# Late softmax probabilities moved by way of DRAM instead of from SBUF to SBUF

## The chip, the cores and the metric

The kernel runs on one core of one Trainium2 chip. The metric is device microseconds of one execution; lower is better.

## The reference

Three layers follow one another over 4 x 576 = 2304 tokens of 512 numbers. The first is attention with 8 heads, half of them with a local mask and half with a strided one, the second a dense squared-ReLU layer, the third a layer of 8 experts of which each token uses one:

```python
scores = np.where(masks, scale * q @ k.T, -1e9)     # local: 32 back; strided: same position mod 32
attn = softmax(scores) @ v                          # (B, H, S, D) = (4, 8, 576, 64)
x = attn.transpose(0, 2, 1, 3).reshape(2304, 512)
h = np.maximum(x @ w_in, 0.0)                       # 512 -> 2048
x = (s * (h * h) + b) @ w_out                       # 2048 -> 512
e = argmax(x @ w_gate, axis=1)                      # one expert per token
out = p[e] * sigmoid(x @ w_output_gate)[e] * (relu(x @ w1[e]) @ w2[e])   # 512 -> 1024 -> 512
```

## The kernel before

All work is written as generators (`attn`, `moe1`, `load_qkv` and so on). A planner, `Order.run`, keeps a clock for each engine, looks at which step could start first by its estimated cost and its rank (the `prio` of `spawn`; a lower number goes first), and so writes one fixed list of instructions for each engine. On the chip every engine runs its list in order and waits on semaphores. The constants such as `DMA_LAT` and `PH_LAT` are the planner's guesses of when a transfer lands; they set the order and no wait.

Tokens are cut into five units (256, 512, 512, 512, 512). Attention is cut into 23 rounds (`GROUPS`). Rounds 0 to 8 come first (lines 591 to 757) and are followed by the dense layer of unit 0; rounds 9 to 22, the late ones, are laid between the products of the dense layer (L1095 into `h`, L1129 from `g`), so that TensorE always has something to do. A late round is one visit on TensorE: 16 products of probabilities with v (L884, from `phs`), and right behind them the scores of the round two further on (L799). Those scores go through the mask (L818), the maximum (L842), the exponentials on ScalarE (L849), the division (L855) and 32x32 transposes on VectorE (L859) into the one tile `prt`. From there the blocks have to come to other partitions, in the one tile `phs`, which has its zeros from the start. In the kernel before, eight DMAs of 32 KB, from SBUF to SBUF, do this (four in rounds of half width); they may start when the products of the round before have read `phs`.

All DMAs of the kernel but a few are issued by SyncE (SP), in the order of its list: also the loads of q, k (`qkv`, 128 x 1088) and v (128 x 1024) of the late rounds, which have one buffer each, the raw weights of the dense layer (`raw64`, in 64-bit words), and `xp`, in which the partial result of a unit is put aside (L1512) and fetched back (L1520) through one tile `x1`. A wait in front of one of them holds up all that stand behind it.

At the start, while attention has not filled TensorE yet, the generator `warm` puts in products of zeros, whose result nobody reads. From L1091 on TensorE works without them.

Of the kernel before, what the change touches and what calls it, by code (L numbers as in the profile page):

```python
# [6 lines left out]
F32 = mybir.dt.float32  # L7
# [29 lines left out]
P = 128  # L37
STRIDE = 32
QB = 64
# [13 lines left out]
NPR = 2  # L53
QG = 32
NQE = 6
P_CHAIN = -0.35
P_ATT = -0.3
# [17 lines left out]
P_ATT2 = 0.1  # L75
# [45 lines left out]
def dims(g):  # L121

    if GROUPS[g][0] == "L":
        return (QB, LK) if g < NEARLY else (QG, 2 * QG)
    j0, j1, r = part_of(g)
    if g >= NEARLY:
        return r * (j1 - j0), r * j1
    return r * (j1 - j0), QB if GROUPS[g][0] == "P" else r * j1


def span(g):
    kind, b, i0, n = GROUPS[g]
    if kind == "L":
        return b * S + i0 * QB, b * S + (i0 + n) * QB
    j0, j1, _ = part_of(g)
    return b * S + j0 * STRIDE, b * S + j1 * STRIDE
# [61 lines left out]
LAT = 0.25  # L198
DMA_LAT = 1.8
LATE_LAT = 0.8  # L200
PH_LAT = 0.8
BIG = 180


# [112 lines left out]
def op(*engs, waits=(), dep=True, on=(), late=0.0):  # L317
    return engs, waits, dep, on, late
# [6 lines left out]
def body(ctx, tc, qkv, w12, moe_s, moe_b, wg, e12, out):  # L325
    nc = tc.nc
# [5 lines left out]
    dram = enter(tc.tile_pool(name="dram", bufs=1, space=DRAM))  # L332
# [23 lines left out]
    prs = [at.tile([P, 1024 // 2], F32, name=f"pr{k}", tag=f"pr{k}", bufs=1) for k in range(NPR)]  # L356
    prt = at.tile([P, 1024 // 2], F32, name="prt", tag="prt", bufs=1)
    phs = at.tile([P, 2, 2, 256], F32, name="phs", tag="phs", bufs=1)
    away = at.tile([P, 2, USZ[AWAY]], F32, name="away", tag="away", bufs=1)
    mh = wp.tile([P, sum(MB[0])], F32R, name="mh", tag="w")  # L360
    x0 = wp.tile([P, KD, USZ[0]], F32, name="x0", tag="w")
# [26 lines left out]
    zero = xk["S"][:, 1, 1, COL["S"][2]:COL["S"][2] + 2 * P]  # L388
# [6 lines left out]
    o = Order()  # L395
# [68 lines left out]
    t_qe, t_qk, t_vv, t_pt, t_ph = Tok(NQE), Tok(1), Tok(1), Tok(1), Tok(1)  # L464
# [108 lines left out]
    for g, (kind, b, i0, n) in enumerate(GROUPS):  # L573
        t0, t1 = span(g)
# [229 lines left out]
    def late_mask(g, sc, toks):  # L804
        kind, b, i0, n = GROUPS[g]
        local = kind == "L"
        nq, w = dims(g)
        m = 2 * n
        sm = at.tile([P, 24], F32, name="sm", tag="sm", bufs=NSM)
        ps4 = prs[g % NPR][:, 0:m * 2 * QG].rearrange("p (h i k) -> p h i k", h=2, k=2 * QG)[:, :, :, 0:w]  # L810
        edge = [i for i in range(n) if local and (i0 + i) % NLB == 0]
        some = [(i, i + 1, ml[:, 2 * QG:4 * QG]) for i in edge]
        for i, j in zip([0] + [i + 1 for i in edge], edge + [n]):
            if i < j:
                some.append((i, j, ml[:, 0:2 * QG] if local else late_m[kind, b]))
        yield op(("DVE", m * w / 960 + 0.15 * len(some)), on=toks)
        for i, j, mask in some:
            nc.vector.tensor_tensor(out=ps4[:, :, i:j], in0=sc[:, :, i:j], in1=mask.unsqueeze(1).unsqueeze(1).to_broadcast([P, 2, j - i, w]), op=ALU.add)  # L818
        o.spawn(late_rest(g, sm, ps4), prio=P_ATT2, pe=P_ATT)

    def attn_late(g):
        n = GROUPS[g][3]
# [9 lines left out]
    def late_rest(g, sm, ps4):  # L832
        kind, b, i0, n = GROUPS[g]
        local = kind == "L"
        nq, w = dims(g)
        m = 2 * n
# [8 lines left out]
        for h in range(2):  # L845
            for i in range(n):
# [10 lines left out]
        nb = 2 if w > QG else 1  # L857
        yield op(("DVE", nb * m * QG / 960 + 0.15), waits=[t_pt])
        nc.vector.transpose(out=prt[:, 0:nb * m * QG].rearrange("p (b c q) -> p b c q", b=nb, q=QG),  # L859
                            in_=pr[:, 0:m * 2 * QG].rearrange("p (c b q) -> p b c q", b=2, q=QG)[:, 0:nb])  # L860
        o.free(t_p)
        yield op(("DMA", 2.55 * nb), waits=[t_ph])
        for x in range(2):
            for y in range(nb):
                for p in range(2):
                    a, r = p * QB + x * QG, x * QB + y * QG
                    nc.sync.dma_start(out=phs[r:r + QG, p, x, 0:m * QG], in_=prt[a:a + QG, y * m * QG:(y + 1) * m * QG])
        t1 = o.fin + DMA_LAT + PH_LAT
        o.free(t_pt, t1)
        ev = Ev()  # L870
        o.set(ev, t1)
        tot = m * nq
# [7 lines left out]
        for i in range(n):  # L880
            for p in range(2):
                for h in range(2):
                    c = (h * n + i) * QG
                    nc.tensor.matmul(out=two[h * D:(h + 1) * D, p, 256 + 2 * i * nq:256 + 2 * (i + 1) * nq], lhsT=vv[:, i, p, h, :],  # L884
                                     rhs=phs[:, p, :, c:c + nq])
        o.free(t_vv)
        o.free(t_ph)
        if nx:
# [3 lines left out]
        for t0, c, z, _ in segs:  # L892
            if local:
                a = t0 - span(g)[0]
# [7 lines left out]
        for z, src, dst, u in runs:  # L902
            if u == AWAY:
# [9 lines left out]
                if local:  # L913
                    a = span(g)[0] - UOF[AWAY]
# [13 lines left out]
        if nx:  # L928
            yield from late_mask(nx, sc, toks)
# [1370 lines left out]
    def extra(col, get, n=NT):  # L2300
        yield op(("DMA", 4.2), waits=[ev_gid])
        e = get()
        gr = mx.tile([1, SLOT], I32, name="gr", tag="gr", bufs=1)
        gc = mx.tile([P, 2], I32, name="gc", tag="gc", bufs=1)
        with nc.allow_non_contiguous_dma(reason="one column of a table"):
            nc.sync.dma_start(out=gr, in_=col(gid).rearrange("s o -> o s"))
            for h in range(NROW):
                nc.sync.dma_start(out=gc[h * SLOT:(h + 1) * SLOT, 0:1], in_=col(gid))
            nc.sync.dma_start(out=gc[0:SLOT, 1:2], in_=col(sid))
        t_gr = Ev()  # L2310
        o.set(t_gr, o.fin + 3.0)
        yield op(("DVE", 0.4), waits=[t_gr])
        gs = mx.tile([P, 3], I32, name="gs", tag="gs", bufs=1)
        nc.vector.tensor_single_scalar(out=gs[:, 0:1], in_=gc[:, 0:1], scalar=P - 1, op=ALU.bitwise_and)
        nc.vector.tensor_single_scalar(out=gs[:, 1:2], in_=gc[:, 0:1], scalar=P.bit_length() - 1, op=ALU.logical_shift_right)
        nc.vector.scalar_tensor_tensor(out=gs[:, 2:3], in0=gs[:, 0:1], scalar=float(NQT), in1=gs[:, 1:2], op0=ALU.mult, op1=ALU.add)
        yield op(("POOL", 1.1))
        se = mx.tile([P, 1], F32, name="se", tag="se", bufs=1)
        nc.gpsimd.indirect_dma_start(out=se, out_offset=None, in_=scd,
                                     in_offset=bass.IndirectOffsetOnAxis(ap=gs[:, 2:3], axis=0))  # L2320
        src = mx.tile([P, KD, NT], F32, name="X1", tag="big", bufs=1)
        for u in range(NU):
            yield op(("DMA", USZ[u] / 180), waits=[ev_last[u], ev_raw])
            nc.sync.dma_start(out=src[:, :, UOF[u]:UOF[u + 1]], in_=xd[u])
        ev = Ev()
        o.set(ev, o.fin + DMA_LAT + 1.0)
        yield op(("DVE", 1.8), waits=[t_r, ev])
        xe = mx.tile([P, KD, SLOT], F32, name="xe", tag="r", bufs=NR)
        for k in range(0, SLOT, 4):
            if k:  # L2330
                yield op(("DVE", 0.8))
            _, vs = nc.values_load_multi_w_load_instructions(
                gr[0:1, k:k + 4], engines=[DVE], min_val=0, max_val=NT - 1, skip_runtime_bounds_check_because=why)
            for j, v in enumerate(vs):
                nc.vector.tensor_copy(out=xe[:, :, k + j:k + j + 1], in_=src[:, :, bass.ds(v, 1)])
        big = mx.tile([P, NF2, 1024], F32, name="we", tag="big", bufs=1)
        we = []
        evs = []
        for fc in range(NF2):
            yield op(("DMA", 1.46))  # L2340
            t = big[:, fc, :]
            nc.sync.dma_start(out=t, in_=e12[bass.ds(e * NF2 + fc, 1)].rearrange("o p f -> p (o f)"))
            we.append(t)
            evs.append(Ev())
            o.set(evs[-1], o.fin + DMA_LAT)
        if n < NT:
            yield op(("DMA", 0.5))
            ex["lrow"] = const.tile([1, P], I32, name="lrow")
            nc.sync.dma_start(out=ex["lrow"], in_=lsd.rearrange("(o s) c -> o (s c)", o=1))
        if n < NT:  # L2350
            oe = yield from rows_fast(xe, we, evs, se)
        else:
            oe = rows_short(xe, big, se)
        ex["oe"], ex["gc"] = oe, gc
        if n < NT:
            yield from merge_rows(oe, gc)
        yield op(("POOL", 1.1), waits=list(ev_out))
        nc.gpsimd.indirect_dma_start(out=out[0:n], out_offset=bass.IndirectOffsetOnAxis(ap=gc[0:SLOT, 1:2], axis=0),
                                     in_=oe, in_offset=None, bounds_check=n - 1, oob_is_err=False)
        o.free(t_g)  # L2360
# [13 lines left out]
    def warm():  # L2374
        yield op(("PE", 0.0), waits=[t_l1])
        t = ps.tile([P, 512], F32, name="warm", tag="l1")
        n = 0
        while ev_x[0].t is None and n < WARM:
            yield op(("PE", 0.155), dep=False)
            nc.tensor.matmul(out=t[:, 0:2 * P], lhsT=zero[:, 0:P], rhs=zero)  # L2380
            n += 1
        o.free(t_l1)

# [126 lines left out]
```

## Time and profile before

| what | value |
|---|---|
| time, median of 3 runs | 663.77 us (661.78 to 665.29) |
| the profiled execution's own time | 662.37 us |
| its span, first to last instruction | 660.6 us |
| TensorE busy | 651.9 us, 99% of the span |
| VectorE, ScalarE busy | 426.6 us, 312.8 us |
| mean granted TensorE clock | 0.997 |
| DMA share, first slices and mean GB/s | 0.8 to 0.9 in the first two slices of 40; 127 GB/s over the span |

The span is 1.77 us shorter than the execution's own time. "Busy" on TensorE counts a product from its start to its modelled end, so that products that overlap are counted once; an engine that is busy for 99% of the span has hardly any moment without a product under way.

### The profile page before, as it was taken

Reading aid. Unit: us, or ns where it says so; the run is one execution under the profiler, and the core shown is the slowest. Engines: PE = TensorE matmul, PEld = TensorE weight load, DVE = VectorE, ACT = ScalarE, POOL = GpSimd, SP = SyncE. Lnnn points to the kernel's source line nnn. Section 1 sums busy time; section 2 is a strip of 40 time slices with the busy share of each in tenths; the row PEclk is TensorE's granted clock in tenths of the full one; section 3 lists DMA queues with packets and bytes.
Section 4 is the critical chain, followed back from the end, with each engine's and each line's share of the span. In section 5 each row is a group of like instructions: output and inputs, shape, how many; then the busy total and the mean of one; then the engine's idle time right before and its main releaser. Section 6 shows DMA issues by size and latency. Waiting matters only on the chain. (4 is left out here: it accounts for less than half of the span.)

```text
span 660.6 us, 14155 instructions
## 1 busy us (share of the span) xinstructions
PE 651.9 (99%) x5424; PEld 570.0 (86%) x5424; DVE 426.6 (65%) x1001; ACT 312.8 (47%) x848; POOL 38.8 (6%) x135
## 2 busy tenths in 40 slices
PE   7999999999999999999999999999999999999997
PEld 6888888899878888898899889988899999998996
DVE  5898868776545557566575767887687566535540
ACT  4876865677566444353243464543322423314311
POOL 7650000000000000000000000000000000000000
PEclk9999999999999999999999999999999999999999
DMA  8982356673544232112211242333220660910201
GB/s 312 405 334 96 112 209 208 207 245 103 177 152 169 81 106 65 49 48 97 87 50 42 64 152 68 116 97 96 96 65 2 177 237 14 327 44 16 81 1 66
DMA packets 40823, 83.81 MB, mean 127 GB/s; under 512 B 6701, under 2 KB 20142, under 8 KB 39986
## 3 DMA queue, kind: packets, MB, share of 16 engines
q1 hardware_dynamic: 40658, 82.87, 37.2%
q8 instruction: 43, 0.70, 0.5%
q14 instruction: 26, 0.21, 0.1%
q0 software_dynamic: 96, 0.02, 0.0%
HBM read 64.11 MB, written 15.63 MB: 121 GB/s over the span
## 5 line engine op out<-in xcount | busy, mean ns | idle before, releaser
L1095 PE MATMUL h<-xsl,w 128*128 128x512 f32 (+1 forms) x492 | 109.5, 369 | 0.0
L1129 PE MATMUL bk<-g,w 128*128 128x512 f32 (+1 forms) x480 | 105.5, 368 | 0.0
L1190 PE MATMUL bk<-g,w 128*128 128x512 f32 x396 | 102.2, 393 | 0.0
L1095 PEld LDWEIGHTS h<-xsl,w 128*128 128x128 f32 x492 | 84.8, 188 | 15.6 <-issue 0.4
L1968 PE MATMUL bk<-w,ht 128*128 128x512 f32 x384 | 96.0, 391 | 0.0
L1129 PEld LDWEIGHTS bk<-g,w 128*128 128x128 f32 x480 | 83.0, 188 | 14.7
L1190 PEld LDWEIGHTS bk<-g,w 128*128 128x128 f32 x396 | 69.9, 188 | 11.6
L1968 PEld LDWEIGHTS bk<-w,ht 128*128 128x128 f32 x384 | 68.6, 188 | 11.6
L1043 ACT ACTIVATE r<-h 128x512 f32<-128x512 f32 (+1 forms) x48 | 25.3, 528 | 62.5 <-PE h L1095 59.5
L1069 DVE TENSOR_TENSOR g<-r,g 128x512 fp32r<-128x512 f32 (+1 forms) x41 | 26.0, 633 | 42.6 <-ACT g L1067 42.2
L1442 PEld LDWEIGHTS h<-xsl,w 128*128 128x128 f32 x336 | 45.5, 190 | 3.8 <-issue 0.2
L1442 PE MATMUL h<-xsl,w 128*128 128x256 f32 x336 | 47.0, 283 | 0.0
L1873 ACT ACTIVATE ht<-h 128x256 fp32r<-128x256 f32 x24 | 9.2, 385 | 73.2 <-PE h L2010 47.0
L849 ACT ACTIVATE pr<-pr,sm 128x64 f32<-128x64 f32 (+2 forms) x102 | 32.8, 322 | 0.3
L1914 DVE TENSOR_TENSOR dd<-h,su 128x256 f32<-128x256 f32 x16 | 6.8, 424 | 29.5 <-PE h L2010 29.4
L1356 ACT ACTIVATE g<-dd 128x512 fp32r<-128x512 f32 x16 | 10.1, 631 | 31.5 <-DVE dd L1349 31.5
L1067 ACT ACTIVATE g<-r 128x512 fp32r<-128x512 f32 (+1 forms) x41 | 23.9, 583 | 1.7
L1055 ACT ACTIVATE r<-r 128x512 f32<-128x512 f32 (+1 forms) x41 | 23.9, 584 | 1.1
L2010 PE MATMUL bk<-x,wc 128*128 128x256 f32 x168 | 24.4, 281 | 0.0
L1442 PE MATMUL h<-xsl,s 128*128 128x256 f32 x168 | 24.3, 279 | 0.0
L1442 PEld LDWEIGHTS h<-xsl,s 128*128 128x128 f32 x168 | 22.6, 188 | 1.3
L1938 ACT ACTIVATE ob<-bk,scl 128x512 f32<-128x512 f32 x17 | 11.7, 689 | 23.5 <-PE bk L1968 22.8
(306 smaller groups left out, 1132.7 us busy)
## 6 DMA issues: line engine op xcount, KB each, us to landing
raw<-w SPq DMA_DIRECT2D x32, 512.0 KB, 6.9
qkv<-qkv SPq DMA_DIRECT2D x14, 512.0 KB, 4.7
xr<-xd SPq DMA_DIRECT2D x9, 512.0 KB, 4.7
qkv<-qkv SPq DMA_DIRECT2D x8, 544.0 KB, 6.3
out<-ob SPq DMA_DIRECT2D x17, 256.0 KB, 2.1
xd<-x SPq DMA_DIRECT2D x4, 1024.0 KB, 4.2
sraw<-sd SPq DMA_DIRECT2D x16, 256.0 KB, 2.7
wraw<-e SPq DMA_DIRECT2D x16, 256.0 KB, 3.0
```

The source lines that it names most:

```text
L849: nc.scalar.activation(out=ps4[:, h, i, :], in_=ps4[:, h, i, :], func=AF.Exp, scale=0.125, bias=v[2][:, j:j + 1], accum_out=v[1][:, j:j + 1])
L1043: nc.scalar.activation(out=r, in_=h, func=AF.Relu)
L1055: nc.scalar.activation(out=to, in_=r, func=AF.Square)
L1067: nc.scalar.activation(out=gt[:, 0, 0:U], in_=r, func=AF.Copy)
L1069: nc.vector.tensor_sub(out=gt[:, 1, 0:U], in0=r, in1=gt[:, 0, 0:U].bitcast(F32))
L1095: nc.tensor.matmul(out=h, lhsT=w_t[2 * fc][:, a, c * P:(c + 1) * P], rhs=xt(u, c, x), start=(c == 0 and n == 0), stop=(c == KD - 1 and n = ...
L1129: nc.tensor.matmul(out=acc[pu][c], lhsT=w_t[2 * pf + 1][:, a, c * P:(c + 1) * P], rhs=gt[:, x, 0:cols(pu)], start=(first and n == 0), stop ...
L1190: nc.tensor.matmul(out=acc[pu][c], lhsT=w_t[2 * pf + 1][:, a, c * P:(c + 1) * P], rhs=pbox[0][:, x, 0:cols(pu)], start=(begin and i == 0), ...
L1442: nc.tensor.matmul(out=out_, lhsT=weights(x, a, c), rhs=o_place(u, b)[y][:, c], start=(first and c == 0 and n == 0), stop=(name in ("M2", ...
L1938: nc.scalar.activation(out=ob, in_=src, func=AF.Copy, scale=scl[:, i:i + 1])
L1968: nc.tensor.matmul(out=acc2[s, t][0], lhsT=box[k][:, x, t * P:(t + 1) * P], rhs=w_t["p", 2 * f + 1][:, a, :], start=(f == 0 and n == 0), s ...
L2010: nc.tensor.matmul(out=banks[to], lhsT=t[:, a, off + c * P:off + (c + 1) * P], rhs=x2[s, b][:, y, c, :], start=(first and c == 0 and n == ...
```

## The change

The late probabilities go from `prt` to a DRAM tile (`ptd`, two of them) in two DMAs, and from there into `phs` in four (two for rounds of half width), whose axes are swapped. The loads wait until the stores have landed. `prt` is free when the stores have landed, and no longer when `phs` has been filled. The planner gets other numbers: two issues at 1.15 us and four at 1.74 us in place of eight at 5.1 us, 0.4 us more for the stores' landing than for a plain one, `PH_LAT` 1.0 for 0.8, 2.0 us more for the landing of the expert weights of the extra rows, and rank -0.1 instead of 0.1 for the work behind the scores of rounds 14 and later. Each warming product of 256 columns becomes two of 128; the planner counts 0.155 us for the pair as it did for the one.

```diff
-PH_LAT = 0.8
+PH_LAT = 1.0
+G_ATT3 = 14
+P_ATT3 = -0.1
+PS_LAT = 0.4
+WE_LAT = 2.0
...
+    ptd = [dram.tile([2, QG, 2, 2, 256], F32, name=f"ptd{k}") for k in range(NPR)]
...
-        o.spawn(late_rest(g, sm, ps4), prio=P_ATT2, pe=P_ATT)
+        o.spawn(late_rest(g, sm, ps4), prio=P_ATT3 if g >= G_ATT3 else P_ATT2, pe=P_ATT)
...
-        yield op(("DMA", 2.55 * nb), waits=[t_ph])
+        yield op(("DMA", 1.15))
+        pd_ = ptd[g % NPR]
+        c = m * QG
+        for p in range(2):
+            nc.sync.dma_start(out=pd_.rearrange("x k b p c -> (x k) b p c")[:, 0:nb, p, 0:c],
+                              in_=prt[p * QB:(p + 1) * QB, 0:nb * c].rearrange("q (b c) -> q b c", b=nb))
+        t1 = o.fin + DMA_LAT + PS_LAT
+        o.free(t_pt, t1)
+        ev = Ev()
+        o.set(ev, t1)
+        yield op(("DMA", 0.87 * nb), waits=[t_ph, ev])
         for x in range(2):
-            for y in range(nb):
-                for p in range(2):
-                    a, r = p * QB + x * QG, x * QB + y * QG
-                    nc.sync.dma_start(out=phs[r:r + QG, p, x, 0:m * QG], in_=prt[a:a + QG, y * m * QG:(y + 1) * m * QG])
+            for b in range(nb):
+                nc.sync.dma_start(out=phs[x * QB + b * QG:x * QB + (b + 1) * QG, x, :, 0:c], in_=pd_[x, :, b, :, 0:c])
         t1 = o.fin + DMA_LAT + PH_LAT
-        o.free(t_pt, t1)
...
-                                     rhs=phs[:, p, :, c:c + nq])
+                                     rhs=phs[:, :, p, c:c + nq])
...
-            o.set(evs[-1], o.fin + DMA_LAT)
+            o.set(evs[-1], o.fin + DMA_LAT + WE_LAT)
...
             yield op(("PE", 0.155), dep=False)
-            nc.tensor.matmul(out=t[:, 0:2 * P], lhsT=zero[:, 0:P], rhs=zero)
+            for c in (0, P):
+                nc.tensor.matmul(out=t[:, c:c + P], lhsT=zero[:, 0:P], rhs=zero[:, c:c + P])
```

In the list of TensorE, the change moves the late rounds among the products of the dense layer and leaves their number as it is. Here is round 10 before (L1095 and L1129 are the dense layer, L884 and L799 the round):

```order
L1095 MATMUL h<-xsl,w 128x512 x12
L1129 MATMUL bk_937<-g,w 128x512 x3
L1129 MATMUL bk_938<-g,w 128x512 x3
L1129 MATMUL bk_939<-g,w 128x512 x3
L1129 MATMUL bk_940<-g,w 128x512 x3
L884 MATMUL bk_1177<-phs,qkv 64x48 x16
L799 MATMUL bk_1177<-qkv 32x64 x32
```

And the same place in the changed kernel, in which L1107 and L1141 are the dense layer, L896 and L804 the round:

```order
L1107 MATMUL h<-xsl,w 128x512 x6
L896 MATMUL bk_1213<-phs,qkv 64x48 x16
L804 MATMUL bk_1213<-qkv 32x64 x32
L1107 MATMUL h<-xsl,w 128x512 x6
L1141 MATMUL bk_973<-g,w 128x512 x3
```

The round now stands 18 products of 512 columns earlier. In the same way round 14 stands in front of one step of L1129 (12 products of 258 columns) and six products of L1095 that were in front of it; the later ones stand up to 36 such products earlier.

In the list of SyncE around round 14, before, v of round 14 and q, k of round 16 (L592) are issued right behind the store of the partial result (L1512), ahead of its fetch (L1520) and of the round's eight moves:

```order
L1512 DMA xp_129<-x_2114 128x2048
L592 DMA qkv<-qkv 128x1024
L592 DMA qkv<-qkv 128x1088
L1520 DMA x_2264<-xp_128 128x4x256
L867 DMA phs<-prt 32x256 x8
```

In the changed kernel (L1524 and L1532 are the store and the fetch, L871 and L880 the round's way through DRAM, L597 the loads of v and of q, k):

```order
L871 DMA ptd_91<-prt 128x1x256 x2
L962 DMA raw_2216<-w 128x1024
L1524 DMA xp_131<-x_2148 128x2048
L880 DMA phs<-ptd_91 32x512 x4
L1532 DMA x_2292<-xp_130 128x4x256
L597 DMA qkv<-qkv 128x1024
L597 DMA qkv<-qkv 128x1088
```

The two loads have moved behind the fetch, which waits until the store has landed.

On ScalarE, ahead of that store, the partial result was evicted by three instructions here and one on VectorE:

```order
L1507 ACTIVATE x_2114<-bk_937,s_sb 128x512
L1507 ACTIVATE x_2114<-bk_938,s_sb 128x512
L1507 ACTIVATE x_2114<-bk_940,s_sb 128x512
L1043 ACTIVATE r<-h 128x256
L1055 ACTIVATE r<-r 128x256
L1067 ACTIVATE g<-r 128x256
L910 ACTIVATE away<-bk_1177 128x32x16
```

In the changed kernel all four stand on ScalarE (L1519), with the first step of the next product's chain (L1055) between them:

```order
L1519 ACTIVATE x_2148<-bk_973,s_sb 128x512
L1519 ACTIVATE x_2148<-bk_974,s_sb 128x512
L1519 ACTIVATE x_2148<-bk_975,s_sb 128x512
L1055 ACTIVATE r<-h 128x256
L1519 ACTIVATE x_2148<-bk_976,s_sb 128x512
L1079 ACTIVATE g<-r 128x256
L922 ACTIVATE away<-bk_1213 128x32x16
```

The fourth eviction now comes behind an instruction that waits for a product.

## Rows read from the trace of the kernel before

**Rows 1.** The cores, and the page's first part: busy us (share) xinstructions.
```profile
core 0: 660.6 us, clock 0.997
PE 651.9 (99%) x5424; PEld 570.0 (86%) x5424; DVE 426.6 (65%) x1001; ACT 312.8 (47%) x848; POOL 38.8 (6%) x135
```

**Rows 2.** TensorE's timeline, start and end: start us, us, instructions [idle before <-releaser].
```profile
1.38 3.35 PE L2380 MATMUL warm<-xsl 128*128 128x256 f32 x14 [1.38 <-DVE xsl L473]
4.54 0.25 PE L632 MATMUL bk<-mk 128*128 128x96 f32 x1
...
6.43 0.98 PE L2380 MATMUL warm<-xsl 128*128 128x256 f32 x6
7.25 0.40 PE L634 MATMUL bk<-mh,mk 128*128 128x256 f32 x2
...
13.87 0.73 PE L639 MATMUL bk<-qkv 64*64 64x96 f32 x24 [1.90 <-DMA qkv<-qkv]
...
18.40 0.86 PE L2380 MATMUL warm<-xsl 128*128 128x256 f32 x5
19.56 0.57 PE L634 MATMUL bk<-mh,mk 128*128 128x324 f32 x2 [0.30 <-ACT x L756]
...
648.57 7.27 PE L2054 MATMUL bk<-w,ht 128*128 128x512 f32 x54
```

**Rows 3.** TensorE's timeline around the late rounds 9 and 14.
```profile
76.29 2.88 PE L1129 MATMUL bk<-g,w 128*128 128x512 f32 x12
79.01 2.88 PE L1095 MATMUL h<-xsl,w 128*128 128x512 f32 x12
81.82 1.15 PE L884 MATMUL bk<-phs,qkv 128*64 128x64 f32 x32
...
149.83 1.62 PE L1129 MATMUL bk<-g,w 128*128 128x258 f32 x12
...
152.09 1.15 PE L884 MATMUL bk<-phs,qkv 128*64 128x64 f32 x32
153.17 0.86 PE L799 MATMUL bk<-qkv 64*32 64x64 f32 x64
```

**Rows 4.** SyncE's timeline: start us, us of issuing, DMAs.
```profile
136.20 0.33 SPq L1512 DMA_DIRECT2D xp<-x  x1
137.87 1.73 SPq L592 DMA_DIRECT2D qkv<-qkv  x2
142.75 0.60 SPq L1520 DMA_DIRECT2D x<-xp  x1
143.89 5.55 SPq L867 DMA_DIRECT2D phs<-prt  x8
```

**Rows 5.** The page's sixth part: DMA issues xcount, KB each, median us to landing.
```profile
phs<-prt SPq DMA_DIRECT2D x96, 32.0 KB, 3.0
...
sd<-sr SPq DMA_DIRECT2D x8, 128.0 KB, 2.2
```

**Rows 6.** ScalarE's timeline at the eviction of the partial result.
```profile
134.36 1.82 ACT L1507 ACTIVATE x<-bk,s_sb 128x512 f32<-128x512 f32 x3
136.42 0.38 ACT L1043 ACTIVATE r<-h 128x256 f32<-128x256 f32 x1 [0.25 <-PE h L1095]
```

**Rows 7.** The tile qkv, loads issued from 137 to 140 us.
```profile
DMA to landing us min/median/max: 6.1/6.4/6.7
```

**Rows 8.** The tile xp, fetch issued at 142.75 us.
```profile
DMA to landing us min/median/max: 5.1/5.1/5.1
```

**Rows 9.** Weight loads by form: busy us, mean ns of one | idle before.
```profile
L884 PEld LDWEIGHTS bk<-phs,qkv 128*64 128x64 f32 x408 | 13.0, 138 | 4.5 <-issue 3.9 <-DVE pr L855 0.4
...
L2393 PEld LDWEIGHTS bk<-xsl 128*128 128x128 f32 x5 | 0.7, 192 | 0.0
```

**Rows 10.** Stretches at the start: us, busy of each engine, PEclk (granted clock), DMA share, GB/s.
```profile
16.00:18.00 2.00, 2.00 (x42) 1.83 (x43) 1.16 (x4) 1.47 (x7) 0.00 (x0) 0.50 1.03 407
18.00:20.00 2.00, 1.70 (x29) 1.28 (x23) 2.00 (x5) 1.78 (x10) 0.00 (x0) 0.94 1.02 401
```

## The prediction

> **What bounds the kernel now.** I read the cores and the page's busy times first. TensorE has a product under way for 651.9 of the 660.6 us [rows 1], at a granted clock of 0.997. It sits idle for 8.7 us in all, and its timeline says where: 1.38 us before the first warming product, 1.90 us at 13.87 for a load of q and k, 0.30 us at 19.56, and the end, since the last products are over at 648.57 + 7.27 = 655.84 and the span lasts 4.76 us longer [rows 2]. These are 8.34 us; 0.36 is left for all other places together. Between 20 and 656 us TensorE is the bound, and it does not wait.
>
> "Busy" could hide slow products, so I look at single blocks. Twelve products of 512 columns take 79.01 - 76.29 = 2.72 us, 227 ns each; with a change to the small products of a late round behind them the same block takes 81.82 - 79.01 = 2.81 us, so a changeover costs 0.09 us [rows 3]. Round 14's products start at 152.09 with no idle note, though their eight moves were issued until 143.89 + 5.55 = 149.44 [rows 3, 4] and land 3.0 us later by the median [rows 5]: they arrive in the moment in which they are wanted, and none of the 14 late rounds stops TensorE. What the change does to SyncE, VectorE and ScalarE therefore pays nothing by itself. It can cost, where something arrives late, and it can move the first 20 us, the only stretch with room.
>
> **The way through DRAM.** Before, the last of eight issues starts seven eighths of 5.55 us, 4.9 us, after the first and lands 3.0 us later: 7.9 us [rows 4, 5]. After: no row shows a store or load of these forms, so I take the same 0.69 us per issue (below: nothing), 2.2 us for a store's landing, as for the 128 KB into `sd`, and 2.0 to 3.0 for the loads (bounds: about the smallest store, and the SBUF moves' median) [rows 5]. The second store starts at 0.7 and lands at 2.9, the last of four loads starts at 5.0 and lands at 7.2 to 8.0. The whole trip is the same length within 0.7 us. The part that must wait until `phs` is free shrinks from 7.9 to four issues and a landing, 5.1 us at most. That is why the rounds can stand earlier. An earlier round saves nothing: the products in front of it are done behind it, 18 times 227 ns = 4.08 us for round 10. Cost and gain: 0. What hides it is the dense layer's products; without this cover each round would show its 5 us.
>
> **What is late next.** The place without room is round 14. Its products move ahead of the block that started at 149.83, so with the changeover they are due at 149.9 [rows 3]. Its v is now issued behind the fetch of the partial result. The fourth eviction stands behind L1055 of the changed list (L1043 before), which ended at 136.42 + 0.38 = 136.80; at 1.82/3 = 0.61 us it ends at 137.4 [rows 6]. SyncE's store then starts at 137.4 in place of 136.20. The fetch came 142.75 - 136.20 = 6.55 us after the store, when that had landed; so now at 143.95. It takes 0.60 us to issue, and v goes at 144.55 [rows 4]. Loads of this size took 6.1 to 6.7 us in that crowded stretch [rows 7], the fetch itself 5.1 [rows 8]. So v lands between 149.65 and 151.25, against 149.9: a wait of 0 to 1.3 us, and I take 0.5. Behind v stand q and k of round 16, issued half of 1.73 us later [rows 4], so landing from 150.5 to 152.1; they are wanted 153.17 - 152.09 = 1.08 us after the start of round 14 [rows 3], at 151.0, and the wait for v covers half of theirs or more. **+0.5** (0 to +1.3). The other edits of numbers, the expert weights' 2.0 us among them, move instructions that TensorE is not waiting for. One group of the extra rows' products (L2241) is cut in two: two more changeovers, **+0.2**.
>
> **The warming products.** There are 34, in groups of 14, 6, 4, 5 and 5. Before, the first 14 took 4.54 - 1.38 = 3.16 us, 226 ns each, and the next six 0.82 us, 122 ns each after the changeover [rows 2]; that is the half and the full level of the clock, though the granted clock is not shown below 1 that early. For a pair of 128 columns no row exists. The lower bound is the same number of columns at the same price, so no change. The upper bound is two products at the old price, twice. The nearest rows are the weight loads: 64 columns took 138 ns, 128 columns 192 [rows 9], so 54 ns per 64 columns, 108 for a load of 128, and each product of these brings its own load. At full level a pair is then 216 ns against 122, at half level 432 against 226. I take this side, as an estimate. The Trainium skill, "TensorE: Matmul & The Clock Gate", section "Wait — 56ns, not 53.3ns?", gives the other: start to start a product costs its columns, 55.6 ns warm and 106.7 cold at 128. By that page a pair would cost 111 or 213 ns, and this term would be about -0.1 us.
>
> With the dear pair: the clock's rise comes with time, at about 4.6, so 7.5 pairs at 0.432 reach 4.6, and 6.5 more at 0.216 end at 6.0 instead of 4.54, 1.5 us late. The 15 pairs of the next three groups add 15 x 0.094 = 1.4. Of these 2.9 us the wait at 13.87 takes 1.9: TensorE is 1.0 us late there. But then it has not been idle before it. Today, after this idle stretch, the granted clock is at 0.50 from 16 to 18 us and back to 0.94 in the next two [rows 10]. Of the 18.40 - 13.87 = 4.53 us some 3.5 lie at the half level; full level would give back up to 1.7, and I take 1.0, since the softmax on VectorE, busy for 2.00 of the two us from 18 on, binds there too [rows 10]. The last five pairs cost 0.5, of which 0.30 is idle time today [rows 2]. Sum: +1.0 - 1.0 + 0.2 = **+0.2**, with -1.7 (the half level gone, the pairs no dearer) and +2.0 (pairs dear, half level stays, and costs double there) as ends.
>
> **The sum.** 660.6 + 0.5 + 0.2 + 0.2 = 661.5 us of span, and with the 1.77 us around it 663.3. That profiled execution (662.37) is 1.4 us below the median of the three runs, 663.77; from the median the same +0.9 gives 664.7. I say 664.0, between.
>
> **Rivals.**
> - The queue on SyncE falls behind (slower). The loads into `phs` wait in order for the stores, and all behind them waits too. For: transfers in the crowded stretch land after 6.1 to 6.7 us [rows 7], not 2.2. Against: only some rounds lie in such stretches, and the trip has room elsewhere. It decides once a store lands some 2 us later than my 2.2 in the rounds from 10 to 16: about five rounds would each stop TensorE by 1 us beyond their room, +5 on 664.0, 669.
> - The pairs are dear and the clock falls all the same: +2.0 in place of +0.2, 666.
> - The pairs cost what one product costs today: the front stays, 663.8. By the page named above this is the case.
> - The clock does not fall and the pairs are cheap: -1.7, so 662.1. The same title, section "What's actually happening", says that throttled is the default and activity lifts it; the trace agrees in that the fall follows the idle stretch of 1.90 us.
> - Faster by over 3.3 us: it would need the whole 1.90 us wait and the whole 1.7 us of half clock back, and nothing lost at round 14. The load at 13.87 is not touched by the change, which speaks against it.
>
> **Chances.** 0.5% of the time is 3.3 us, about what a measurement of this kernel can tell from no change. The forecast with its own range of 662.5 to 665.5 has 0.45, unchanged front 0.17, no fall of the clock 0.13, dear pairs with the fall 0.10, the queue 0.10, faster 0.05. Slower by over 3.3 us (above 667.1) are the queue and a fifth of the dear pairs: 0.12. Faster 0.05, the rest 0.83. From 661.3 to 667.0 the range leaves out the queue, the gain, and little of the others.
>
> **What would show it.** Right: TensorE still busy for 99%, its blocks of twelve at 2.72 us, a wait of at most 1 us in front of round 14's products or the scores behind them, and none in front of the other rounds. The warming pairs: start of the first scores near 6.0 (dear) or still at 4.54 (cheap), and the granted clock from 14 to 20. Wrong: idle notes in front of L896 in many rounds, SyncE waiting long in front of L880, or loads into `phs` that land later than 3 us.

## The result, and the profile after

The changed kernel took 671.34 us (median of 6 runs, 670.27 to 671.52), the kernel before 662.76 us on the same occasions: ratio 1.0121, interval 1.0101 to 1.0141. It is 8.6 us slower. I had forecast 664.0 us, with 661.3 to 667.0 as range, so the measured time is 4.3 us above the upper end of that range. The forecast was about no change; the change is slower, clear of noise.

The first part of the page of the changed kernel, busy us (share) xinstructions, against [rows 1]:

```profile
span 669.7 us, 14153 instructions
PE 663.4 (99%) x5458; PEld 581.0 (87%) x5458; DVE 425.8 (64%) x1000; ACT 311.8 (47%) x849; POOL 38.2 (6%) x135
```

TensorE has 34 products more and is busy for 663.4 - 651.9 = 11.5 us more, and its weight loads (PEld) for 11.0 us more; no other engine has gained work. TensorE's timeline of the changed kernel says where (start us, us, instructions, idle before):

```profile
1.39 6.24 PE L2393 MATMUL warm<-xsl 128*128 128x128 f32 x28 [1.39 <-DVE xsl L478]
7.42 0.39 PE L637 MATMUL bk<-mk 128*128 128x96 f32 x1
...
10.75 2.82 PE L2393 MATMUL warm<-xsl 128*128 128x128 f32 x12
13.37 0.73 PE L639 MATMUL bk<-mh,mk 128*128 128x256 f32 x2
...
15.10 1.97 PE L2393 MATMUL warm<-xsl 128*128 128x128 f32 x8
16.86 1.05 PE L700 MATMUL bk<-mk,pr 128*96 128x128 f32 x4
17.57 2.38 PE L2393 MATMUL warm<-xsl 128*128 128x128 f32 x10
19.87 1.12 PE L730 MATMUL bk<-ph,qkv 96*64 96x64 f32 x16
...
24.65 1.12 PE L700 MATMUL bk<-mk,pr 128*128 128x128 f32 x4
25.41 0.72 PE L639 MATMUL bk<-mk 128*128 128x192 f32 x2
26.07 0.56 PE L644 MATMUL bk<-qkv 64*64 64x96 f32 x16
...
27.07 1.33 PE L2393 MATMUL warm<-xsl 128*128 128x128 f32 x10
...
29.74 1.56 PE L1103 MATMUL h<-x,wf 128*128 128x256 f32 x6
...
657.67 7.27 PE L2066 MATMUL bk<-w,ht 128*128 128x512 f32 x54
```

The same places in the kernel before, where L639 is the L644 of the changed kernel and L1091 its L1103:

```profile
8.20 0.74 PE L2380 MATMUL warm<-xsl 128*128 128x256 f32 x4
9.15 0.61 PE L695 MATMUL bk<-mk,pr 128*96 128x128 f32 x4 [0.21 <-DVE pr L675]
9.52 0.84 PE L2380 MATMUL warm<-xsl 128*128 128x256 f32 x5
10.45 0.69 PE L725 MATMUL bk<-ph,qkv 96*64 96x64 f32 x16
...
16.77 0.92 PE L639 MATMUL bk<-qkv 64*64 64x96 f32 x16
...
20.86 1.99 PE L1091 MATMUL h<-x,wf 128*128 128x256 f32 x8
```

The dense part starts at 29.74 in place of 20.86, 8.88 us late. The last block starts at 657.67, against 648.57 in [rows 2], 9.10 us late. So all but 0.22 us of the loss lies in the first 30 us. There the loss divides like this, up to the scores that start at 26.07 in place of 16.77 (9.30 us late). The first 28 products of 128 columns take 7.42 - 1.39 = 6.03 us, 215 ns each, where 14 of 256 took 3.16 [rows 2]: +2.9. The next 30 (12, 8 and 10) take 2.62 + 1.76 + 2.30 = 6.68 us from their start to that of what follows, where the 15 of 256 (6, 4 and 5) took 0.82 [rows 2] + 0.95 + 0.93 = 2.70: +4.0. The wait of 1.90 us at 13.87 [rows 2] is gone: -1.9. What is left, 9.3 - 2.9 - 4.0 + 1.9 = 4.3 us, is attention at a slower clock: the same products in the same order. The sixteen score products take 0.92 us at 16.77 in the kernel before, where the granted clock is 0.50 [rows 10], and 0.56 at full level, as at 26.07 here. In the changed kernel the four transposes at 24.65 still take 1.12 us; the full level (2.4 GHz) is reached only by 26.07. The granted-clock row prints 1.00 all this time, so that only the durations show the half level (1.2 GHz). Here is one such stretch (us, busy of each engine, granted clock, DMA share, GB/s):

```profile
16.00:18.00 2.00, 2.00 (x11) 1.97 (x12) 1.56 (x5) 0.05 (x1) 0.00 (x0) 1.00 1.01 393
```

The part that I had worried about is quiet. TensorE's waits of the changed kernel (us in total, times, longest) are one line:

```profile
PE warm L2393 <- DVE xsl L478: 1.4, 1, 1.4
```

The timeline at round 14 of the changed kernel, SyncE's first and then TensorE's:

```profile
146.28 0.34 SPq L1524 DMA_DIRECT2D xp<-x  x1
146.81 3.30 SPq L880 DMA_DIRECT2D phs<-ptd  x4
151.41 0.58 SPq L1532 DMA_DIRECT2D x<-xp  x1
152.03 1.09 SPq L597 DMA_DIRECT2D qkv<-qkv  x2
...
158.79 1.15 PE L896 MATMUL bk<-phs,qkv 128*64 128x64 f32 x32
```

SyncE's waits for the stores (us in total, times, longest):

```profile
SPq L880 <- DMA ptd<-prt: 25.4, 14, 4.5
```

and the DMA issues (xcount, KB each, median us to landing):

```profile
ptd<-prt SPq DMA_DIRECT2D x24, 128.0 KB, 2.5
phs<-ptd SPq DMA_DIRECT2D x48, 64.0 KB, 2.0
```

Take the front's 8.88 us off: the store is at 137.40 and round 14 at 149.91, where I had put them at 137.4 and 149.9. SyncE does wait 25.4 us for stores, but no product waits for SyncE.

### The profile page after: what moved, and what is told of

Its sections match the earlier page's. It is cut to its first block, busy times and chain, and to the rows that moved or that the text cites. A ratio compares the mean times of both kernels' runs of the same rounds, so it can differ in the third digit from the quotient of the medians.

```text
span 669.7 us, 14153 instructions
## 1 busy us (share of the span) xinstructions
PE 663.4 (99%) x5458; PEld 581.0 (87%) x5458; DVE 425.8 (64%) x1000; ACT 311.8 (47%) x849; POOL 38.2 (6%) x135
## 5 line engine op out<-in xcount | busy, mean ns | idle before, releaser
L1107 PE MATMUL h<-xsl,w 128*128 128x512 f32 (+1 forms) x492 | 108.5, 368 | 0.0
L1141 PE MATMUL bk<-g,w 128*128 128x512 f32 (+1 forms) x480 | 106.3, 369 | 0.0
L1107 PEld LDWEIGHTS h<-xsl,w 128*128 128x128 f32 x492 | 85.1, 188 | 15.4
L1141 PEld LDWEIGHTS bk<-g,w 128*128 128x128 f32 x480 | 82.8, 188 | 15.0 <-issue 0.2
L1055 ACT ACTIVATE r<-h 128x512 f32<-128x512 f32 (+1 forms) x48 | 25.3, 527 | 74.5 <-PE h L1107 71.6
L2022 PE MATMUL bk<-x,wc 128*128 128x256 f32 x168 | 24.4, 281 | 0.0
```

The lines of the kernel that those rows point to most:

```text
L1055: nc.scalar.activation(out=r, in_=h, func=AF.Relu)
L1107: nc.tensor.matmul(out=h, lhsT=w_t[2 * fc][:, a, c * P:(c + 1) * P], rhs=xt(u, c, x), start=(c == 0 and n == 0), stop=(c == KD - 1 and n = ...
L1141: nc.tensor.matmul(out=acc[pu][c], lhsT=w_t[2 * pf + 1][:, a, c * P:(c + 1) * P], rhs=gt[:, x, 0:cols(pu)], start=(first and n == 0), stop ...
L2022: nc.tensor.matmul(out=banks[to], lhsT=t[:, a, off + c * P:off + (c + 1) * P], rhs=x2[s, b][:, y, c, :], start=(first and c == 0 and n == ...
```

## The experiments

**Theory 1**: the loss is the pairs, by the price of two loads and by a clock that rises late. **Theory 2**: only the price; the clock rises with time. **Theory 3**: the way by DRAM or the new order costs it.

**e1_one_256, e2_pairs_only.** One takes the pairs out of the changed kernel, the other puts them alone into the kernel before:

```diff
-            for c in (0, P):
-                nc.tensor.matmul(out=t[:, c:c + P], lhsT=zero[:, 0:P], rhs=zero[:, c:c + P])
+            nc.tensor.matmul(out=t[:, 0:2 * P], lhsT=zero[:, 0:P], rhs=zero)
```

> The changed kernel with one product of 256 columns in place of each pair of 128; the way by DRAM, the measured landing times, the rank rule and the cut store stay. Theory 1 (the pairs alone cost the 8.6 us: 56 products take 6.0 us where 28 of twice the width would take about as much as a single product each, and the half clock lasts to 25 us): the scores start at about 4.5 us again, the dense part at about 20.9, time 662.5 to 663.5, no difference from before that can be measured. Theory 3 (the way by DRAM or the new order costs it): 669 to 671.

> The kernel before with each warming product of 256 columns made a pair of 128, and nothing else. Theory 1 (the pairs cost it all): about 671, the dense part starts at about 29.7 us. Theory 3 (the way by DRAM or the order): 662.5 to 663.5. If both have a share: between them, and the place where the dense part starts tells the share of the pairs.

Measured: 664.57 us, ratio 1.0029 (1.0018 to 1.0040), without the pairs; 671.27 us, 1.0128 (1.0111 to 1.0145), with the pairs alone, against 662.37. The pairs alone give the whole loss, so theory 3 is not needed for it. The timeline of the kernel with nothing but the pairs:

```profile
1.39 6.24 PE L2381 MATMUL warm<-xsl 128*128 128x128 f32 x28 [1.39 <-DVE xsl L473]
7.42 0.39 PE L632 MATMUL bk<-mk 128*128 128x96 f32 x1
...
28.94 1.99 PE L1091 MATMUL h<-x,wf 128*128 128x256 f32 x8
```

But the changed kernel without them is 2.2 us above before, and I had expected no difference; the two do not add up to the 8.6 us, and the last four experiments take this up.

**e3_half_width.** As many products as before, of half the columns:

```diff
-            nc.tensor.matmul(out=t[:, 0:2 * P], lhsT=zero[:, 0:P], rhs=zero)
+            nc.tensor.matmul(out=t[:, 0:P], lhsT=zero[:, 0:P], rhs=zero[:, 0:P])
```

> The kernel before with one product of 128 columns in place of each one of 256: as many products, half the columns (only products of zeros change). It tells the price of a 128-column product from the effect on the clock. Theory 1 (a product of 128 columns takes as long as one of 256, and the clock rises late): 28 products take about 6 us / 2 = 3.0 as before, the scores start at about 4.5, but the half level lasts beyond 5 us: 664 to 667, the dense part starts at 22 to 25. Theory 2 (only the price is wrong, the rise comes with time at about 4.6 us): 662.5 to 663.5, the dense part at about 20.9.

Measured: 664.42 us, 1.0027 (1.0015 to 1.0039). Its timeline:

```profile
1.39 3.25 PE L2380 MATMUL warm<-xsl 128*128 128x128 f32 x14 [1.39 <-DVE xsl L473]
4.44 0.39 PE L632 MATMUL bk<-mk 128*128 128x96 f32 x1
...
16.24 1.24 PE L639 MATMUL bk<-qkv 64*64 64x96 f32 x24
...
18.23 0.66 PE L695 MATMUL bk<-mk,pr 128*128 128x128 f32 x4
...
22.86 2.00 PE L1091 MATMUL h<-x,wf 128*128 128x256 f32 x8
```

Fourteen products of 128 columns take 4.44 - 1.39 = 3.05 us, 218 ns each, hardly less than fourteen of 256 (226 ns, from [rows 2]). And the half level lasts until about 18 us, though TensorE had products under way without a gap. Theory 2 falls: the price does not differ here from before, and the time does. The two shares can be read off: the late clock costs 664.42 - 662.37 = 2.05 us, what is left of it once the wait at 13.87 is used up (no wait stands at 16.24), and the second product of each step 671.27 - 664.42 = 6.85 us. The rows give about the same: 29 x 0.22 + 5 x 0.13 = 7.0 us; 0.13 is what one of the last ten pairs' products takes at full level, 1.33 us over 10 in the timeline at 27.07 of the changed kernel.

**e7_narrow_weights.** Pairs as in the change, with weights of 32 columns:

```diff
-            nc.tensor.matmul(out=t[:, 0:2 * P], lhsT=zero[:, 0:P], rhs=zero)
+            for c in (0, P):
+                nc.tensor.matmul(out=t[0:32, c:c + P], lhsT=zero[:, 0:32], rhs=zero[:, c:c + P])
```

> The kernel before with each warming product made a pair of 128 columns, with weights of 32 columns (only products of zeros change). If the 215 ns of a product of 128 columns is its weight load (128 columns in rows that took 192 to 333 ns), a product here takes 107 to 120 ns at the half level, the 28 pairs again about 6.0 / 2 = 3.0 us, scores at about 4.5. If 215 ns belongs to the columns that pass through, pairs take 6.0 us as in the changed kernel, scores at 7.4, time 669 to 671. [...]

Measured: 662.49 us, 1.0000 (0.9991 to 1.0009). The timeline of its start:

```profile
1.39 3.19 PE L2381 MATMUL warm<-xsl 128*32 128x128 f32 x28 [1.39 <-DVE xsl L473]
4.38 0.39 PE L632 MATMUL bk<-mk 128*128 128x96 f32 x1
...
5.19 0.56 PE L639 MATMUL bk<-qkv 64*64 64x96 f32 x16
```

Its loads in the view of the tile (ns min/median/max, first and last start):

```profile
L2381 PEld LDWEIGHTS warm<-xsl x68: 106/112/169, 1.4 to 19.0; 128*32 128x32 f32 x68
```

The same loads in the changed kernel:

```profile
L2393 PEld LDWEIGHTS warm<-xsl x68: 186/333/337, 1.4 to 28.1; 128*128 128x128 f32 x68
```

Twenty-eight products now take 2.99 us, 107 ns each, half of 215, and the scores run at the full level from 5.19. So it is not the splitting that costs, it is the second load of 128 columns. The edit narrows the written rows of the output along with the weights, but in e3 half as many columns written per product left the price where it was. And the load's own time at the half level falls from 333 to 169 ns (the median above and the longest of e7) with 96 columns less, which makes some 219 ns for 128 columns (an estimate from these two rows), the spacing that is seen. At the half level such a load sets 215 ns per product where 128 columns need 107, and is hidden behind 256 columns (226). The Trainium skill, "TensorE: Matmul & The Clock Gate", section "Back-to-back issue gap", says that in a stream of loads and products the spacing is set by both. The trace agrees: 107 against 215 ns by the load alone.

**e4_no_warming, e5_fewer_wider, e6b_filled_wait.** All from the kernel before: no products of zeros; half as many, twice as wide; 12 more in front of the wait at 13.87. The three edits, in this order:

```diff
-WARM = 150
+WARM = 0
...
-        o.filler = filler
+        o.filler = None
...
-            nc.tensor.matmul(out=t[:, 0:2 * P], lhsT=zero[:, 0:P], rhs=zero)
+            if n % 2:
+                nc.tensor.matmul(out=t.rearrange("p (k c) -> p k c", k=2), lhsT=zero[:, 0:P],
+                                 rhs=zero.unsqueeze(1).to_broadcast([P, 2, 2 * P]))
...
+        if g == 3:
+            for _ in range(12):
+                nc.tensor.matmul(out=two_banks(toks)[:, 0, 0:2 * P], lhsT=zero[:, 0:P], rhs=zero)
```

> The kernel before without any product of zeros: no warming and no filler at all (only results that nobody reads are left out). It bounds what the warming can be worth, from the other side. The scores then wait for their first load and not for TensorE, and run at the half level until late. If the late rise of the clock and not the 3 us in front of the first scores makes up the loss: the front ends 1 to 4 us later than before, 664 to 667, and still 4 us or more ahead of the changed kernel's 671. If the warming of before is worth nothing, since the loads bind the front: 662 to 663.5.

> The kernel before with one product of 512 columns in place of every second one of 256, none in place of the others: as many columns, half the weight loads (only products of zeros change). The opposite direction of the change. If a product takes the longer of its columns' time and its load: 7 products of 512 take about 3.0 us as the 14 of 256 did, the clock rises at about 5 us, dense part at 20.5 to 21.2, time 661.5 to 663.5. If the number of products matters to the clock: late rise, 664 to 668.

> The kernel before with 12 more products of 256 columns of zeros ahead of round 3's mask products, where TensorE waits 1.90 us for a load today and shows a granted clock of 0.50 to 0.71 from 14 to 18 us. If that half level is what holds the front: no fall, the dense part starts 0.5 to 1.0 us earlier, 661.3 to 662. If the loads hold it, as the look at the kernel with one 256-column product says (clock never fell there, and waits of 1.67 and 0.90 us for q and k stood in its place): dense part at 20.7 to 21.7, 662.3 to 663.5.

Measured, against 662.22: 664.35 (1.0033, 1.0022 to 1.0045), 664.01 (1.0030, 1.0020 to 1.0040) and 663.01 (1.0010, 1.0001 to 1.0019). The first is as expected: the kernel without any warming loses about 2 us, 7 less than the one with pairs. Its timeline:

```profile
10.97 0.69 PE L725 MATMUL bk<-ph,qkv 96*64 96x64 f32 x16 [0.68 <-ACT ph L701]
...
21.18 3.29 PE L1091 MATMUL h<-x,wf 128*128 128x256 f32 x8
```

The products at 10.97 run at the full level; in the changed kernel the same ones, at 19.87, take 1.12 us. So the half level lasted longer behind the pairs than with no products of zeros at all. What this kernel loses comes later: its dense part starts only 0.3 us late but at the half level, 3.29 us for eight products that took 1.99.

The second missed. Its front was even early, with the dense part at 20.45; in its profile TensorE waits 0.3 us for the expert weights at L2241, and from the last VectorE instruction to the end it takes 5.6 us where before took 4.6. The wider products cost nothing at the start; in this execution its loss is not in the front. The third agrees with the second of its two expectations in its time, and there is no gain: with the filled wait the dense part starts at 21.49. But in its profile no product waits for q and k, since the clock rose only near 11 us, so it does not show what holds the front when the clock is up early. The control below does: there it is the loads.

**e8_no_rank_no_we, e9_way_old_order, e10_order_old_way, e11_control.** What are the 2 us of the changed kernel without pairs? One takes out the rank and the longer landing of the expert weights; one has the way by DRAM alone, with the old lists; one the new order alone, with the eight old moves; one is the kernel before with an empty line added. The cores of their edits, first that of e8 against e1:

```diff
-G_ATT3 = 14
+G_ATT3 = 99
-WE_LAT = 2.0
+WE_LAT = 0.0
```

then that of e9 against the kernel before (with `phs`'s axes swapped as in the change). e10 is the same exchange the other way round in e1, with `prt` freed behind the moves:

```diff
         yield op(("DMA", 2.55 * nb), waits=[t_ph])
-        for x in range(2):
-            for y in range(nb):
-                for p in range(2):
-                    a, r = p * QB + x * QG, x * QB + y * QG
-                    nc.sync.dma_start(out=phs[r:r + QG, p, x, 0:m * QG], in_=prt[a:a + QG, y * m * QG:(y + 1) * m * QG])
+        pd_ = ptd[g % NPR]
+        c = m * QG
+        for p in range(2):
+            nc.sync.dma_start(out=pd_.rearrange("x k b p c -> (x k) b p c")[:, 0:nb, p, 0:c],
+                              in_=prt[p * QB:(p + 1) * QB, 0:nb * c].rearrange("q (b c) -> q b c", b=nb))
+        for x in range(2):
+            for b in range(nb):
+                nc.sync.dma_start(out=phs[x * QB + b * QG:x * QB + (b + 1) * QG, x, :, 0:c], in_=pd_[x, :, b, :, 0:c])
```

> The kernel with the way by DRAM and one 256-column product, but without the higher rank of the later rounds and without the 2.0 us more for the expert weights. The kernel with both was at 664.57, 1.0029 of before. If the rank or the cut at the expert weights causes that 1.9 us: 662.4 to 663.3 here, and the extra 0.2 us at the expert weights gone. If the way by DRAM or the front is the cause: 664.0 to 665.0, with the front's 0.75 us still there.

> The kernel before with only the way by DRAM: the two stores and four loads stand where the eight moves stood, the lists of TensorE, VectorE and ScalarE are those of before, row for row. The two kernels with the way by DRAM and 256-column warming were 1.9 to 2.0 us slower than before (1.0029, 1.0031). If the way itself causes it: 664 to 665. If the new order of the dense part causes it: 662 to 663. If it is a matter of how one program's front and last store happen to fall: anywhere between.

> The new order (the changed kernel's lists of TensorE and VectorE, row for row; 12 rows of ScalarE's differ), with one 256-column warming product and with the eight moves from SBUF to SBUF in place of the way by DRAM. If the order causes the 1.9 us: 664 to 665. If the way by DRAM does: 662 to 663.3; but in the new order the rounds stand up to 18 products earlier, and the moves took 7.9 us where the trip takes less in its last part, so waits in front of the late rounds' products of up to 1 us each may add 0 to 5: then 663 to 668, with idle notes at L896.

> The kernel before, with an empty line added and nothing else. It tells how far a comparison of equal programs strays, and shows the front and the last store of one more execution: 661.5 to 663, ratio 0.999 to 1.001. The clock's rise may come anywhere from 5 to 9 us, as in the four executions of the same front so far, and the end of the span 4.6 to 6.1 us after the last VectorE instruction.

Measured: 664.23 (1.0031, 1.0019 to 1.0043, against 662.22); then, against 662.61, 665.29 (1.0055, 1.0034 to 1.0077; its 12 runs spread from 662.97 to 669.86), 665.17 (1.0041, 1.0025 to 1.0057) and, for the control, 662.15 (0.9997, 0.9986 to 1.0007). So the rank and the expert weights are not the cause, and equal programs agree to 0.1%. The way in the old order and the order with the old way each cost some 2.6 us by their medians; together they cost 2.2. With the way in the old order one round waits for `phs`, 0.5 us.

The new order with the old moves, TensorE's timeline at round 14:

```profile
150.24 0.34 PE L892 MATMUL bk<-phs,qkv 128*64 128x64 f32 x4 [0.42 <-DMA phs<-prt]
150.86 1.04 PE L892 MATMUL bk<-phs,qkv 128*64 128x64 f32 x28 [0.29 <-DMA phs<-prt]
153.28 0.86 PE L803 MATMUL bk<-qkv 64*32 64x64 f32 x64 [1.38 <-DMA qkv<-qkv]
```

and with the way by DRAM (e1):

```profile
150.58 1.15 PE L896 MATMUL bk<-phs,qkv 128*64 128x64 f32 x32
151.87 0.86 PE L804 MATMUL bk<-qkv 64*32 64x64 f32 x64
```

With the old moves the rounds wait for `phs` and, behind the moves on SyncE, for q and k; with the way by DRAM the scores start 151.87 - 150.58 = 1.29 us after the round, against 1.08 in [rows 3], so 0.2 us is lost. The way by DRAM makes the earlier order possible. But TensorE was not waiting before, so the order pays nothing.

The control's front, TensorE's timeline:

```profile
13.04 0.73 PE L640 MATMUL bk<-qkv 64*64 64x96 f32 x24 [0.43 <-DMA qkv<-qkv]
...
16.44 0.56 PE L640 MATMUL bk<-qkv 64*64 64x96 f32 x16 [1.10 <-DMA qkv<-qkv]
...
20.00 0.79 PE L640 MATMUL bk<-qkv 64*64 64x108 f32 x24 [0.89 <-DMA qkv<-qkv]
20.71 1.99 PE L1092 MATMUL h<-x,wf 128*128 128x256 f32 x8
```

In this execution the clock did not fall after 14 us (the sixteen score products take 0.56 us, not 0.92), and three shorter waits for q and k stand in place of one: the dense part starts at 20.71, within 0.15 us of 20.86. So the fall of the clock in [rows 10] costs next to nothing: without it TensorE waits for the loads instead.

Of the 2.2 us without pairs the one profiled execution shows 0.76 in the front (dense part at 21.62, three waits for q and k, 3.1 us in all), 0.3 around rounds 14 and 16, and 0.3 at L2253; its end comes 1.4 us later behind the last VectorE instruction than that of before (6.1 us against 4.6). The front differs as much between two profiles of one code (before and the control), and the end takes 4.6 to 6.1 us in the profiles of all these kernels, whose last lines of code are the same; which part of the 2 us recurs stays open.

## Why the prediction was wrong, point by point

- **The warming products: the step that failed.** I wrote "the clock's rise comes with time, at about 4.6" and summed the term to +0.2, with +2.0 as its upper end. Shown: with the pairs the half level lasts to about 24 us in e2 and to 26 in the changed kernel. Products of 128 columns at the old number (e3) hold it to 18. So 29 pairs were paid at 0.43 to 0.46 us, where I had put 6.5 of the first 14 and the next 15 at 0.216. The term measured +8.9 (e2).
- **The price of a pair was right.** 432 ns at the half level was my estimate; it is 2 x 215 = 430. The value of the Trainium skill that stood against it, 106.7 ns for 128 columns ("TensorE: Matmul & The Clock Gate", section "Wait — 56ns, not 53.3ns?"), is met with weights of 32 columns (107 ns, e7) and not with 128 (215).
- **"It has not been idle before it", so full level gives back 1.0.** The idle time did go; the clock had not risen at all, so nothing came back. And the control shows that there was nothing to give: with the clock full the loads take its place.
- **The upper end** was made for a clock that falls at 13.87; the case "dear and never up" was not among the rivals. Pairs at 0.432 throughout against my own rows give 14 x (0.432 - 0.226) + 15 x (0.432 - 0.122) = 7.5 us before the attention is counted and the wait taken off. This was to be had from the rows; I did not work it out, since I took the time at which the clock rose before for a property of the chip, where it was one of what TensorE was doing.
- **The way through DRAM, cost and gain 0: right in the changed kernel.** The stores land after 2.5 us (2.2 taken), the loads after 2.0, no round waits. This holds behind a front that is 8.9 us late. With the front in its place the same kernel is 2.2 us above before (e1), and how much of that is the way stays open; that 664.57 is close to my 664.0 is luck, since the sum had no term for it.
- **Round 14, +0.5 (0 to 1.3): right mechanism, size 0.** In the changed kernel v is issued at 152.03, lands 4.4 us later, where I had taken 5.1 to 6.7, and is wanted at 158.79; the fetch came 5.13 us behind the store and not 6.55. Where the front is not late (e1) q and k cost 0.2.
- **L2241 cut in two, +0.2: right in kind, 0.3 measured.** From its first product to the block `h<-xa,wa` behind it (L2022, L2010 before) it is 594.18 - 589.07 = 5.11 us, where before took 585.06 - 580.28 = 4.78. The 0.22 over all that follows the front has 0.1 of gain elsewhere in it.
- **The rival "the queue on SyncE falls behind"** would also have ended slower, and it is not what happened: SyncE waits, TensorE does not.

No version here beats the kernel before. e7 equals it.

## What to carry to other kernels

Before a product is split, look at what loads its weights: here a load of 128 columns hid behind 256 columns (226 ns) and not behind 128 (215 ns), and two halves then cost two wholes. A clock that rises early in one profile does so after what TensorE did there; where a change alters that work, the price is to be worked out for the case that the rise does not come, for everything up to the next stretch of other work. And an order that brings work forward pays nothing on an engine that waits for nothing.

## What was not expected of the hardware

- Products under way without a gap did not raise the clock: 17 us of them (e3) and 24 us of them (changed kernel) at the half level. The Trainium skill, "TensorE: Matmul & The Clock Gate", section "What's actually happening", says that the warm-up is a matter of time and not of the number of products; the traces here differ, and behind the wider products it rose at 4.6 to 11 us in equal code, behind the pairs with narrow weights (e7) at about 5.
- The granted-clock row shows 1.00 in those stretches.
- The rise in code that is equal up to it came at about 4.6 us (before), 6.0 (control) and near 11 us (e8), with the dense part at 20.86, 20.71 and 20.32. Up to there a late rise costs next to nothing: it takes time that TensorE otherwise spends waiting for q and k, 1.9 us before, 2.4 in the control and none in e8.
